# Moving part of the gate matrix onto three DMA engines, and the last pieces of wo back to full rows

## The chip, the cores and the metric

One core of a Trainium2 chip. The metric is the device time of one execution in microseconds (us); the kernel is timed in several executions beside the other kernel on the same chip. A profile shows one execution; its span is some 1.3 us shorter than the time on the clock (194.8 against 196.06 in the profile of the kernel before). On one core there is no second die to compare with, so a run is called fast when it lies within 1.5% of the fastest of its kernel.

## The reference

One decoding step: attention over the last 4,096 positions of a K and a V cache, beside a gated feed-forward layer, mixed by a gate g.

```python
def _A_ref(x, k_cache, v_cache, wq, wo):              # x: 4 x 1 x 512
    q = (x @ wq).reshape(B, Sq, 32, 128)...           # wq: 512 x 4096
    k = k_cache[:, :, Sk - 4096:, :]                  # 4 x 8 x 4096 x 128, bf16: 33.5 MB; v the same
    p = softmax(q k^T * Dh ** -0.5); o = p v
    return o.reshape(B, Sq, 4096) @ wo                # wo: 4096 x 512

def _B_ref(x, W_gate, W_up, W_down):                  # 512 x 1792, 512 x 1792, 1792 x 512
    gate = x @ W_gate; up = x @ W_up
    return (relu(gate) * up) @ W_down

g = sigmoid((x * gate_w).sum(-1))
return g * _A_ref(x, ...) + (1 - g) * _B_ref(x, ...)
```

Every byte of K, V and the five matrices is read once: 81.0 MB.

## The kernel before

Everything goes through four 4 MiB slots of the on-chip memory in one fixed order of loads, all issued by SP: wq, x, gate_w, K0, K1, V0, then K and V of the eight sets in turn, the gate and up matrices, the last V, the down matrix, and wo in five pieces. DVE transposes K, PE makes scores and PV (the weighted sums of V). PE is the matrix engine, DVE the vector engine, ACT the scalar engine; SP only issues loads. At the end PE does, in this order: the last PV, the down projection (`hg`), `fold` (16 matmuls that add up and regroup the attention output), and, once DVE has made `oq` from it, 64 matmuls with wo. The last 64 KB of wo are cut into loads of 123, 3 and 2 partitions, which leave eight completion marks (191.87 to 192.39) where a load of all 128 partitions leaves sixteen. Their packets of 512 B run in three trains, about 23.7 ns apart in each, so they are taken to go onto three DMA engines only; these are called the low three below. The sixteen marks of a full load lie close together at first (22.30 to 22.84 for the first K). The parts that the change touches:

```python
WO_PIECES = ((0, 34), (34, 52), (52, 60), (60, 63), (63, 64))   # in units of 256 columns, 64 KB each
LOW3 = (0, 123, 126, 128)

def _dma_order():
    o = [("wq",), ("x",), ("gw",), ("k", 0), ("k", 1), ("v", 0)]
    for s in range(2, NSET):
        o += [("k", s), ("v", s - 1)]
    return o + [("wg",), ("wu",), ("v", NSET - 1), ("wd",)] + [("wo", p) for p in range(len(WO_PIECES))]

    def wo_rows(p):      # the last piece in three loads of 123, 3 and 2 partitions
        return [slice(a, b) for a, b in zip(LOW3, LOW3[1:])] if p == len(WO_PIECES) - 1 else [slice(0, 128)]
# ... sync:
            elif k == "wg":
                load(("WG",), "d_wg", Wg, B_W_gate.rearrange("(p t) f -> p (t f)", t=4), waits=w)
            elif k == "wo":
                lo, hi = WO_PIECES[it[1]]
                wo = A_wo.rearrange("(p i) c -> p (i c)", i=32)
                for n, r in enumerate(wo_rows(it[1])):
                    load(("WO", it[1], n), f"d_wo{it[1]}", Wo[r, OW * lo:OW * hi], wo[r, OW * lo:OW * hi], waits=w)
# ... tensor:
        def XT():        # x and gate_w transposed, four 5-column pieces
            for q in range(4):
                tp(bk[:, 6 * q:6 * q + 5], xsb[0:5, q:q + 509:4], identb[0:5, 0:5], ...)
        def GU():        # gate and up: four row groups q, four column blocks j of 448
            for n, (W, key) in enumerate(((Wg, "WG"), (Wu, "WU"))):
                for q in range(4):
                    for j in range(4):
                        mm(banks[scb(fill)][32 * j:32 * j + 4, 0:448], xT[:, 5 * q:5 * q + 4],
                           W[:, FF * q + 448 * j:FF * q + 448 * j + 448], q == 0, q == 3, ...)
        def WO(p):
            for x in range(lo, hi):
                mm(banks[ACC][OR * j:OR * j + 4, 0:OW], oq[:, i, :], Wo[:, OW * x:OW * x + OW], False, i == 31,
                   waits=w if x == lo else (), ...)
# ... vector and scalar evict one half of the output each:
        def FIN():       # DVE waits for the last piece, ACT for the last but one
            E.op(lambda: v.tensor_copy(osum[:, OW:2 * OW], banks[ACC][OR:OR + 4, 0:OW]), ...)
```

Of the kernel before, what the change touches and what calls it, by code (L numbers as in the profile page):

```python
# [16 lines left out]
FF = 1792  # L17
# [7 lines left out]
OUTT = 2  # L25
OW = 512 // OUTT
OR = 128 // OUTT
WO_PIECES = ((0, 34), (34, 52), (52, 60), (60, 63), (63, 64))
LOW3 = (0, 123, 126, 128)

class _Plan:

# [70 lines left out]
def _alloc(nc, ctx):  # L103
    R = {}

    def sb(name, shape, dt):
        R[name] = ctx.enter_context(nc.sbuf_tensor(name, shape, dt))

    sb("slots", [128, NSLOT, 16384], BF16)
    sb("kt", [128, 4, 4096], BF16)  # L110
    sb("sc", [128, 2048], BF16)
    sb("pe", [128, 2048], BF16)
    sb("pT", [128, 2, 2048], BF16)
    sb("qblk", [128, NSET, 2, 144, 2], BF16)
    sb("xsb", [5, 512], BF16)
    sb("xT", [128, 20], BF16)
    sb("osb", [128, NSET, 512], BF16)
    sb("oq", [128, 32, 4], BF16)
    sb("identb", [128, 128], BF16)
    sb("identf", [128, 128], FP32)  # L120
    sb("ones", [128, 128], FP32)
    sb("ee", [16, 128], BF16)
    sb("e4", [16, 128], BF16)
    sb("rfold", [128, 128], FP32)
    sb("grpb", [128, 128], BF16)
    sb("own8", [128, 8], FP32)
    sb("scl", [128, 8], FP32)
    sb("maskl", [128, 128], BF16)
    sb("maskr", [128, 512], BF16)
    sb("maskf", [128, 512], BF16)  # L130
    sb("gwB", [128, 4, 128], BF16)
    sb("fold", [128, 4, 4, 64], BF16)
    sb("mx4", [128, 4], FP32)
    sb("rd32", [128, 8, 4], BF16)
    sb("negmax", [128, 2], FP32)
    sb("rowsum", [128, NSET], FP32)
    sb("recip", [128, 4, 4], FP32)
    sb("ge", [128, 2, 4], FP32)
    sb("gp", [128, 2, 4], FP32)
    sb("gg", [128, 2, 4], FP32)  # L140
    sb("hg", [128, 14, 4], BF16)
    sb("osum", [4, 512], BF16)
    R["psum"] = ctx.enter_context(nc.psum_tensor("bank", [128, 8, 512], FP32))
    return R

# [11 lines left out]


def _dma_order():
    o = [("wq",), ("x",), ("gw",), ("k", 0), ("k", 1), ("v", 0)]  # L160
    for s in range(2, NSET):
        o += [("k", s), ("v", s - 1)]
    return o + [("wg",), ("wu",), ("v", NSET - 1), ("wd",)] + [("wo", p) for p in range(len(WO_PIECES))]


def _slots():

    frees = [[] for _ in range(NSLOT)]
    at, wait = {}, {}
    turn = 0  # L170
    for it in _dma_order():
        k = it[0]
        if k in ("x", "gw") or (k == "wo" and it[1] > 0):
            continue
        if k == "wu":
            at[it] = at[("wg",)]
            wait[it] = wait[("wg",)]
            continue
        n = turn % NSLOT
        turn += 1  # L180
        at[it] = n
        wait[it] = list(frees[n])
        frees[n] = {"k": [("E", "KT", it[-1], 3)], "v": [("PV", it[-1])], "wq": [("Q", 1)], "wg": [("GU", 1)], "wd": [], "wo": []}[k]
    return at, wait


def _program(nc, plan, R, aps):
# [5 lines left out]
    xsb, xT, osb, oq = R["xsb"], R["xT"], R["osb"], R["oq"]  # L193
    identb, identf, ones = R["identb"], R["identf"], R["ones"]
    mx4, rd32, negmax, rowsum, recip = R["mx4"], R["rd32"], R["negmax"], R["rowsum"], R["recip"]
    ge, gp, gg, osum = R["ge"], R["gp"], R["gg"], R["osum"]
    consts = {"mask": R["maskf"], "grp": R["grpb"], "rfold": R["rfold"]}

    at, slot_wait = _slots()
# [39 lines left out]
        n = scf[key] - NSC  # L239
        return [("E",) + sck[n]] if n >= 0 else [("INIT",)]  # L240

    def wo_rows(p):

        return [slice(a, b) for a, b in zip(LOW3, LOW3[1:])] if p == len(WO_PIECES) - 1 else [slice(0, 128)]

    def set_of(s):
        return s % 4, s // 4
# [4 lines left out]
    def sync(e):  # L252
# [5 lines left out]
        for it in _dma_order():  # L258
# [6 lines left out]
            elif k == "wq":  # L265
                load(("WQ",), "d_wq", slot("wq"), A_wq.rearrange("(p t) f -> p (t f)", t=4), waits=w)
            elif k == "wg":
                load(("WG",), "d_wg", Wg, B_W_gate.rearrange("(p t) f -> p (t f)", t=4), waits=w)
            elif k == "wu":
                load(("WU",), "d_wu", Wu, B_W_up.rearrange("(p t) f -> p (t f)", t=4), waits=w)  # L270
            elif k == "wd":
# [2 lines left out]
            elif k == "wo":  # L274
                lo, hi = WO_PIECES[it[1]]
                wo = A_wo.rearrange("(p i) c -> p (i c)", i=32)
                for n, r in enumerate(wo_rows(it[1])):
                    load(("WO", it[1], n), f"d_wo{it[1]}", Wo[r, OW * lo:OW * hi], wo[r, OW * lo:OW * hi], waits=w)
            else:
                b, qq = set_of(it[1])  # L280
                src = (A_k_cache if k == "k" else A_v_cache)[b, 4 * qq:4 * qq + 4, SK - WIN:SK, :]
                load((k.upper(), it[1]), f"d_{k}{it[1] % 3}", slot(*it), src.rearrange("h (r c) d -> r h (c d)", r=32),
                     waits=w)
# [32 lines left out]
    def tensor(t):  # L316
# [16 lines left out]
        def XT():  # L333
            bk = bankb[tr(("XT",))]
            for q in range(4):
                tp(bk[:, 6 * q:6 * q + 5], xsb[0:5, q:q + 509:4], identb[0:5, 0:5], ev=("XT",) if q == 3 else None,
                   waits=tr_free(("XT",)) + [("X",), ("GW",), ("IDB",)])

        def Z():
            for q in range(4):  # L340
# [65 lines left out]
        def GU():  # L406
            for n, (W, key) in enumerate(((Wg, "WG"), (Wu, "WU"))):
                fill = ("GU", n)
                for q in range(4):
                    for j in range(4):  # L410
                        mm(banks[scb(fill)][32 * j:32 * j + 4, 0:448], xT[:, 5 * q:5 * q + 4],
                           W[:, FF * q + 448 * j:FF * q + 448 * j + 448], q == 0, q == 3,
                           ev=fill if (q, j) == (3, 3) else None, pos=(0, 32 * j),
                           waits=sc_free(fill) + [(key,)] if (q, j) == (0, 0) else ())

        def FFN():
            for i in range(14):
# [5 lines left out]

        def WO(p):
            lo, hi = WO_PIECES[p]
            w = [("WO", p, n) for n in range(len(wo_rows(p)))] + [("E", "OQ")]
            for x in range(lo, hi):
                i, j = x // OUTT, x % OUTT
                mm(banks[ACC][OR * j:OR * j + 4, 0:OW], oq[:, i, :], Wo[:, OW * x:OW * x + OW], False, i == 31,
# [8 lines left out]
    for it in order:  # L438
# [3 lines left out]
        elif k == "CONST":  # L442
            act.append(("ECONST", it[1]))
        elif k == "XT":
            dve.append(("EXT",))
            act.append(("GWB",))
        elif k == "Z":
            act.append(("GE",))
# [33 lines left out]
    def vector(v):  # L482
        E = _Eng(plan, v, "dve")

        def INIT():
            E.op(lambda: v.memset(qblk[:, :, :, :, :].rearrange("p s h c e -> p (s h c e)"), 0.0), ev=("QZ",))  # L486
            E.op(lambda: v.memset(R["psum"][:, SCB[0]:ACC + 1, :].rearrange("p k c -> p (k c)"), 0.0), ev=("INIT",))

        def EKT(s, f):
            w = [("K", s)] + ([("SC", s - 1, f)] if s else [])  # L490
            E.op(lambda: v.transpose(kt[:, f, :].bitcast(FP32), slot("k", s)[:, 4096 * f:4096 * f + 4096].bitcast(FP32)),  # L491
                 ev=("E", "KT", s, f), waits=w)

        def EXT():
            E.op(lambda: v.tensor_copy(xT[:, :].rearrange("p (q c) -> p q c", q=4), bankb[tr(("XT",))][:, 0:24].rearrange("p (q c) -> p q c", q=4)[:, :, 0:5]), ev=("E", "XT"), waits=[("XT",)])  # L495

        def EQ(n):
            key = ("Q", n)
# [41 lines left out]

        def EPT(s):
            E.op(lambda: v.transpose(pT[:, s % 2, :], pe[:, :]), ev=("E", "PT", s),  # L542
                 waits=[("EXP", s)] + ([("PV", s - 2)] if s >= 2 else []))

        def ERS(g):
            key = ("RS", g)
# [29 lines left out]
        def FIN():  # L576
            E.op(lambda: v.tensor_copy(osum[:, OW:2 * OW], banks[ACC][OR:OR + 4, 0:OW]), ev=("OSUM", 1),  # L577
                 waits=[("WOP", len(WO_PIECES) - 1)])

        fns = dict(INIT=INIT, EKT=EKT, EXT=EXT, EQ=EQ, G=G, EQT=EQT, ESC=ESC, MAX=MAX, ESW=ESW, EPT=EPT, ERS=ERS, EOQ=EOQ, H=H,  # L580
                   EHT=EHT, FIN=FIN)
        for it in dve:
            fns[it[0]](*it[1:])
# [1 line left out]
    def scalar(a):  # L585
# [35 lines left out]

        def FIN():
            E.op(lambda: a.activation(osum[:, 0:OW], banks[ACC][0:4, 0:OW], ACTF.Copy), ev=("OSUM", 0),
                 waits=[("WOP", len(WO_PIECES) - 2)])

        fns = dict(ECONST=ECONST, GWB=GWB, EQ=EQ, GE=GE, RELU=RELU, EXP=EXP, NORM=NORM, FIN=FIN)
        for it in act:
# [31 lines left out]
```

## Time and profile before

| | before |
|---|---|
| time, median of 3 | 196.12 us (196.02 to 196.21) |
| span of the profile, granted TensorE clock | 194.8 us, 0.912 |
| data moved, rate over the span | 81.01 MB, 416 GB/s |
| DMA queue's share of sixteen engines' span | 97.3% |
| busy: PE, DVE, ACT | 62%, 64%, 14% |

The prediction below shows the page, the end of the chain of waits and the PE timeline of the tail. The waits (engine and line, what it waited for, total us, times, longest us):

```profile
DVE kt L491 <- DMA slots<-in_A_k_cache_dram: 28.0, 6, 5.2
PE bank L320 <- DMA slots<-in_A_v_cache_dram: 5.7, 1, 5.7
```

DVE has 28 us in which it waits for K: it has slack, DMA has none. The second line is PE waiting for the last V, at the end. What PE then does, in the timeline (start, duration, engine, line, operation):

```profile
178.49 5.03 PE L320 MATMUL bank<-slots,pT 128*64 128x512 bf16 x32 [5.70 <-DMA slots<-in_A_v_cache_dram]
183.45 1.69 PE L320 MATMUL bank<-slots,hg 128*4 128x256 bf16 x28
185.07 1.93 PE L320 MATMUL bank<-osb,fold 128*64 128x256 bf16 x16
...
187.04 0.88 DVE L555 TENSOR_TENSOR oq<-bank,recip 64x128 bf16<-64x128 f32 x2 [12.25 <-PE bank L320]
188.05 1.75 PEld L320 LDWEIGHTS bank<-slots,oq 128*4 128x4 bf16 x34 [1.31 <-DMA slots<-in_A_wo_dram]
```

A third reading is not a view but the trace's completion marks: a load of all 128 partitions leaves sixteen as it lands, as many as the page counts DMA engines, and so a mark is read here as one engine's part that has landed. A load that leaves fewer has one more soon after SP has issued it (at 8.67 us for the first side load, whose issue ended at 8.25), which is not counted. Marks carry no engine's name: that two loads met on one engine is read from which marks come late. They are quoted in us from the span's start, and a mark's place is where it stands in their order. An instruction page (often just a page) is a packet of 16,384 B on queue q8, which the profile lists as instruction (5 packets, 0.08 MB, in the kernel before); the prediction shows when they come.

### The profile page before, as it was taken

How to read it: one execution, taken by the hardware profiler on the slowest of the kernel's cores; microseconds unless marked ns; L12 is line 12 of the kernel's file. 1: busy time of each engine (PE TensorE's matmuls, PEld its weight loads, DVE VectorE, ACT ScalarE, POOL GpSimd, SP SyncE). 2: the span in 40 equal slices, each digit the busy share in tenths (PEclk: the TensorE clock that was granted, in tenths of full speed). 3: DMA queues.
4: the chain of work that ended last, by engine and by line, in shares of the span. 5: the costliest groups of instructions: out<-in, count | busy, mean ns of one | idle time of the engine just before them, and what ended most of it. 6: DMA issues, size and time to landing. Idle time of an engine off the chain costs nothing.

```text
span 194.8 us, 1734 instructions
## 1 busy us (share of the span) xinstructions
PE 120.6 (62%) x723; PEld 50.6 (26%) x723; DVE 124.1 (64%) x153; ACT 27.5 (14%) x34; POOL 9.5 (5%) x25
## 2 busy tenths in 40 slices
PE   0209279474943894686468943894586466743974
PEld 0003123121411341242112411341142122311562
DVE  6103769999399809980998199819981998370010
ACT  2213000040130013001300130013001300420100
POOL 7830000000000000000000000000000000000000
PEclk9999958999999797899876999697999889997899
DMA  6999999999999999999999999999999999999992
GB/s 215 431 432 431 437 437 431 431 427 451 431 437 437 446 427 424 431 437 431 431 431 431 427 424 437 444 437 431 431 431 421 431 395 427 470 431 384 425 404 90
DMA packets 3616, 81.10 MB, mean 416 GB/s; under 512 B 401, under 2 KB 666, under 8 KB 794
## 3 DMA queue, kind: packets, MB, share of 16 engines
q1 hardware_dynamic: 3610, 81.01, 97.3%
q8 instruction: 5, 0.08, 0.2%
q14 instruction: 1, 0.01, 0.0%
HBM read 81.01 MB, written 0.00 MB: 416 GB/s over the span
## 4 chain that ended last, share of the span: by engine, by line
DMA 54%; DVE 31%; PE 9%; issue 4%; SPq 0%; ACT 0%
DMA slots<-in_A_k_cache_dram 38%; DVE kt L491 21%; DMA slots<-in_A_wo_dram 10%; PE bank L320 7%; DMA xsb<-in_A_x_dram 6%; DVE sc L527 5%; DVE qblk L517 1%; PE bank L324 1%; DVE pT L542 1%; DVE rd L531 1%; SPq L256 0%; DVE negmax L537 0%; ACT gwB L600 0%; DVE osum L577 0%; DVE mx L527 0%
## 5 line engine op out<-in xcount | busy, mean ns | idle before, releaser
L491 DVE STREAM_TRANSPOSE kt<-slots 128x2048 f32<-128x2048 f32 x32 | 73.7, 2305 | 28.1 <-DMA slots<-in_A_k_cache_dram 28.0
L320 PE MATMUL bank<-kt,qblk 128*128 128x512 bf16 x256 | 72.1, 434 | 27.9 <-DVE kt L491 27.9
L320 PEld LDWEIGHTS bank<-kt,qblk 128*128 128x128 bf16 x256 | 25.2, 107 | 69.7 <-DVE kt L491 36.0
L320 PE MATMUL bank<-slots,pT 128*64 128x512 bf16 x256 | 32.3, 410 | 5.7 <-DMA slots<-in_A_v_cache_dram 5.7
L619 ACT ACTIVATE pe<-sc,negmax 128x2048 bf16<-128x2048 bf16 x8 | 16.0, 2002 | 60.1 <-DVE negmax L537 60.1
L527 DVE CUSTOM_DVE_ANT_0 sc<-bank,maskf 128x512 bf16<-128x512 f32 x32 | 21.0, 658 | 3.8 <-PE bank L320 3.7
L320 PEld LDWEIGHTS bank<-slots,pT 128*64 128x64 bf16 x256 | 15.1, 118 | 23.2 <-issue 13.4
L542 DVE STREAM_TRANSPOSE pT<-pe 128x2048 bf16<-128x2048 bf16 x8 | 18.5, 2312 | 2.2 <-ACT pe L619 2.2
L604 ACT ACTIVATE osb<-bank 128x512 bf16<-128x512 f32 x8 | 4.8, 597 | 81.5 <-PE bank L320 81.5
L320 PE MATMUL bank<-rd,grpb 128*128 128x32 bf16 x8 | 1.6, 194 | 22.1 <-DVE rd L531 22.1
L555 DVE TENSOR_TENSOR oq<-bank,recip 64x128 bf16<-64x128 f32 x2 | 0.9, 434 | 12.3 <-PE bank L320 12.2
L320 PEld LDWEIGHTS bank<-rd,grpb 128*128 128x128 bf16 x8 | 0.8, 98 | 25.7 <-DVE rd L531 25.7
L495 DVE COPY xT<-bank 128x20 bf16<-128x20 bf16 x1 | 0.2, 171 | 8.0 <-PE bank L324 8.0
L320 PE MATMUL bank<-slots,oq 128*4 128x256 bf16 x64 | 4.0, 272 | 2.0 <-DMA slots<-in_A_wo_dram 2.0
L320 PE MATMUL bank<-slots,xT 128*4 128x512 bf16 (+1 forms) x64 | 5.0, 467 | 0.0
L320 PE MATMUL bank<-maskr,maskl 128*128 128x512 bf16 x1 | 0.6, 609 | 5.9 <-POOL maskr L296 5.9
L517 DVE TENSOR_SCALAR qblk<-bank 32x64 uint32<-32x64 uint32 x16 | 2.9, 215 | 2.1 <-PE bank L324 2.1
L324 PE MATMUL bank<-identb,xsb 5*128 5x5 bf16 x4 | 0.3, 168 | 5.7 <-DMA xsb<-in_A_x_dram 5.7
L577 DVE CAST osum<-bank 4x256 bf16<-4x256 f32 x1 | 0.4, 418 | 5.2 <-PE bank L320 5.2
L320 PEld LDWEIGHTS bank<-slots,oq 128*4 128x4 bf16 x64 | 2.5, 84 | 3.5 <-DMA slots<-in_A_wo_dram 2.9
L296 POOL TENSOR_SCALAR_AFFINE_SELECT fold<-fold 128x256 bf16<-128x256 bf16 x8 | 3.3, 417 | 1.1
L486 DVE MEMSET qblk<- 128x2304 uint32 x1 | 2.0, 1978 | 1.3 <-PEq L644 1.3
(59 smaller groups left out, 40.3 us busy)
## 6 DMA issues: line engine op xcount, KB each, us to landing
slots<-in_A_k_cache_dram SPq DMA_DIRECT2D x8, 4096.0 KB, 25.1
slots<-in_A_v_cache_dram SPq DMA_DIRECT2D x8, 4096.0 KB, 30.5
slots<-in_A_wq_dram SPq DMA_DIRECT2D x1, 4096.0 KB, 12.4
slots<-in_A_wo_dram SPq DMA_DIRECT2D x1, 2176.0 KB, 17.1
slots<-in_B_W_gate_dram SPq DMA_DIRECT2D x1, 1792.0 KB, 19.7
slots<-in_B_W_up_dram SPq DMA_DIRECT2D x1, 1792.0 KB, 23.6
slots<-in_B_W_down_dram SPq DMA_DIRECT2D x1, 1792.0 KB, 18.5
slots<-in_A_wo_dram SPq DMA_DIRECT2D x1, 1152.0 KB, 19.5
```

The source lines that it names most:

```text
L296: op(lambda: e.affine_select(dst, src, pattern, cmp, fill, base=base, channel_multiplier=mult), ev)
L320: E.op(lambda: t.matmul(out_, lhsT, rhs, start=start, stop=stop, tile_position=pos, skip_group_check=True), ev=ev, waits=waits)
L324: E.op(lambda: t.transpose(out_, in_, idn), ev=ev, waits=waits)
L486: E.op(lambda: v.memset(qblk[:, :, :, :, :].rearrange("p s h c e -> p (s h c e)"), 0.0), ev=("QZ",))
L491: E.op(lambda: v.transpose(kt[:, f, :].bitcast(FP32), slot("k", s)[:, 4096 * f:4096 * f + 4096].bitcast(FP32)), ev=("E", "KT", s, f), waits=w)
L517: E.op(lambda dst=dst, r=r, g=g: v.tensor_scalar(dst, src[r, g, 0:B, :, :], 0, None, op0=ALU.bitwise_or), ev=("E",) + keys[1] if (q, g) == ...
L527: E.op(lambda: v.tensor_tensor_reduce(sc[:, 512 * f:512 * f + 512], banks[scb(key)], R["maskf"][:, :], 1.0, -3.0e38, ALU.add, ALU.max, mx4 ...
L531: E.op(lambda: v.tensor_tensor(rd32[:, :, :], bc(R["own8"][:, :].unsqueeze(2), 2, 4), bc(mx4[:, :].unsqueeze(1), 1, 8), ALU.mult), ev=("MA ...
L542: E.op(lambda: v.transpose(pT[:, s % 2, :], pe[:, :]), ev=("E", "PT", s), waits=[("EXP", s)] + ([("PV", s - 2)] if s >= 2 else []))
L555: E.op(lambda g=g, r=r: v.tensor_tensor(oq[r, :, :].rearrange("p i b -> p b i"), banks[tr(key)][0:64, 128 * g:128 * g + 128].rearrange("p ...
L604: E.op(lambda: a.activation(osb[:, s, :], ob(s), ACTF.Copy), ev=("NORM", s), waits=[("PV", s)])
L619: E.op(lambda: a.activation(pe[:, :], sc[:, :], ACTF.Exp, bias=negmax[:, s % 2:s % 2 + 1], scale=SCALE, accum_out=rowsum[:, s:s + 1]), ev= ...
```

## The change

Its intent, as the marks suggest: by the end some engines are late and others early, and the early ones can be given more. An equal load cannot do that, but the loads of 123, 3 and 2 partitions left eight marks, and loads laid out in rows of 3, 3 and 2 were meant to do the same. So 448 columns of one row in four of the gate matrix (114,688 B) are taken out of the equal load and put on three engines early on; in return wo's last 64 KB go back to all sixteen, in full rows. PE then needs the matching rows of x, hence the extra copies, transposes and gate matmuls.

```diff
-WO_PIECES = ((0, 34), (34, 52), (52, 60), (60, 63), (63, 64))
-LOW3 = (0, 123, 126, 128)
+SIDE_F, SIDE_J = 1344, 6
+SIDE = ((3, 5, 0, 0, 0), (3, 5, 60, 32, 0), (2, 1, 120, 0, 5))   # engines, rows each partition, first row, partition, place
+WO_PIECES = ((0, 35), (35, 52), (52, 59), (59, 62), (62, 64))
...
-    o = [("wq",), ("x",), ("gw",), ("k", 0), ("k", 1), ("v", 0)]
+    o = [("wq",), ("x",), ("gw",), ("k", 0), ("side", 0), ("side", 1), ("side", 2), ("k", 1), ("v", 0)]
...
+        e, j, p, q, j0 = SIDE[n]
+        src = wg_all[p:p + 4 * e * j, 3 * FF + SIDE_F:4 * FF]
+        return side[q:q + 4 * e, j0:j0 + j, :], src.rearrange("(r e) f -> e r f", e=e)
...
-                load(("WG",), "d_wg", Wg, ...)
+                load(("WG",), "d_wg", Wg[:, 0:3 * FF + SIDE_F], wg_all[:, 0:3 * FF + SIDE_F], waits=w)
+            elif k == "side":
+                load(("SIDE", it[1]), f"d_side{it[1]}", *side_of(it[1]), waits=[("SZ",)])
...
+            for j in range(SIDE_J):
+                tp(bk[:, 6 * (4 + j):6 * (4 + j) + 5], xg[:, j, :], identb[0:5, 0:5], ...)
...
-                for q in range(4):
+                for q in range(4 if n else 3 + SIDE_J):      # block j = 3 of the last group comes from side, six matmuls
...
+            E.op(lambda: v.memset(xg, 0.0), ev=("XGZ",))
+            E.op(lambda: v.memset(side[...].bitcast(FP32), 0.0), ev=("SZ",))
...  # ACT's half of the output now waits for the last piece, as DVE's does;
...  # hg and osum move into gwB and xsb to make room (cut)
```

More of the change, by code (lines that the diff above doesn't have):

```diff
@@ L115, in _alloc @@
     sb("xsb", [5, 512], BF16)
-    sb("xT", [128, 20], BF16)
+    sb("xT", [128, 20 + 5 * SIDE_J], BF16)
+    sb("side", [128, SIDE_J, FF - SIDE_F], BF16)
     sb("osb", [128, NSET, 512], BF16)
@@ L140, in _alloc @@
     sb("gg", [128, 2, 4], FP32)
-    sb("hg", [128, 14, 4], BF16)
-    sb("osum", [4, 512], BF16)
+    R["hg"] = R["gwB"][:, 0, 0:56].rearrange("p (i b) -> p i b", i=14)
     R["psum"] = ctx.enter_context(nc.psum_tensor("bank", [128, 8, 512], FP32))
@@ L172, in _slots @@
         k = it[0]
-        if k in ("x", "gw") or (k == "wo" and it[1] > 0):
+        if k in ("x", "gw", "side") or (k == "wo" and it[1] > 0):
             continue
@@ L195, in _program @@
     mx4, rd32, negmax, rowsum, recip = R["mx4"], R["rd32"], R["negmax"], R["rowsum"], R["recip"]
-    ge, gp, gg, osum = R["ge"], R["gp"], R["gg"], R["osum"]
+    ge, gp, gg, side = R["ge"], R["gp"], R["gg"], R["side"]
+    osum = xsb[0:4, :]
+    xg = pT[0:5, 0, 0:128 * SIDE_J].rearrange("p (j q) -> p j q", j=SIDE_J)
     consts = {"mask": R["maskf"], "grp": R["grpb"], "rfold": R["rfold"]}
@@ L240, in sc_free, with side_of, side_x @@
         return [("E",) + sck[n]] if n >= 0 else [("INIT",)]
-    def wo_rows(p):
-        return [slice(a, b) for a, b in zip(LOW3, LOW3[1:])] if p == len(WO_PIECES) - 1 else [slice(0, 128)]
+    wg_all = B_W_gate.rearrange("(p t) f -> p (t f)", t=4)
+    def side_of(n):
+        e, j, p, q, j0 = SIDE[n]
+        src = wg_all[p:p + 4 * e * j, 3 * FF + SIDE_F:4 * FF]
+        return side[q:q + 4 * e, j0:j0 + j, :], src.rearrange("(r e) f -> e r f", e=e)
+    def side_x(n):
+        e, j, p, q, j0 = SIDE[n]
+        src = xsb[0:5, 4 * p:4 * p + 16 * e * j].rearrange("p (r j e t) -> p j e r t", r=4, j=j, e=e, t=4)[:, :, :, :, 3]
+        return xg[:, j0:j0 + j, q:q + 4 * e].rearrange("p j (e r) -> p j e r", e=e), src
     def set_of(s):
@@ L267, in sync @@
             elif k == "wg":
-                load(("WG",), "d_wg", Wg, B_W_gate.rearrange("(p t) f -> p (t f)", t=4), waits=w)
+                load(("WG",), "d_wg", Wg[:, 0:3 * FF + SIDE_F], wg_all[:, 0:3 * FF + SIDE_F], waits=w)
+            elif k == "side":
+                load(("SIDE", it[1]), f"d_side{it[1]}", *side_of(it[1]), waits=[("SZ",)])
             elif k == "wu":
@@ L276, in sync @@
                 wo = A_wo.rearrange("(p i) c -> p (i c)", i=32)
-                for n, r in enumerate(wo_rows(it[1])):
-                    load(("WO", it[1], n), f"d_wo{it[1]}", Wo[r, OW * lo:OW * hi], wo[r, OW * lo:OW * hi], waits=w)
+                load(("WO", it[1]), f"d_wo{it[1]}", Wo[:, OW * lo:OW * hi], wo[:, OW * lo:OW * hi], waits=w)
             else:
@@ L335, in XT @@
             for q in range(4):
-                tp(bk[:, 6 * q:6 * q + 5], xsb[0:5, q:q + 509:4], identb[0:5, 0:5], ev=("XT",) if q == 3 else None,
+                tp(bk[:, 6 * q:6 * q + 5], xsb[0:5, q:q + 509:4], identb[0:5, 0:5],
                    waits=tr_free(("XT",)) + [("X",), ("GW",), ("IDB",)])
+            for j in range(SIDE_J):
+                tp(bk[:, 6 * (4 + j):6 * (4 + j) + 5], xg[:, j, :], identb[0:5, 0:5], ev=("XT",) if j == SIDE_J - 1 else None,
+                   waits=[("XG",)])
         def Z():
@@ L408, in GU @@
                 fill = ("GU", n)
-                for q in range(4):
+                for q in range(4 if n else 3 + SIDE_J):
                     for j in range(4):
-                        mm(banks[scb(fill)][32 * j:32 * j + 4, 0:448], xT[:, 5 * q:5 * q + 4],
-                           W[:, FF * q + 448 * j:FF * q + 448 * j + 448], q == 0, q == 3,
-                           ev=fill if (q, j) == (3, 3) else None, pos=(0, 32 * j),
-                           waits=sc_free(fill) + [(key,)] if (q, j) == (0, 0) else ())
+                        of_side = n == 0 and q > 2 and 448 * j >= SIDE_F
+                        if q > 3 and not of_side:
+                            continue
+                        c = 5 * q + 5 * of_side
+                        x = 448 * j - SIDE_F
+                        rhs = side[:, q - 3, x:x + 448] if of_side else W[:, FF * q + 448 * j:FF * q + 448 * j + 448]
+                        last = q == (2 + SIDE_J if of_side else 3)
+                        w = sc_free(fill) + [(key,)] if (q, j) == (0, 0) else []
+                        if n == 0 and (q, j) == (3, 0):
+                            w = [("SIDE", g) for g in range(len(SIDE))]
+                        mm(banks[scb(fill)][32 * j:32 * j + 4, 0:448], xT[:, c:c + 4], rhs, q == 0, last,
+                           ev=fill if last and j == 3 else None, pos=(0, 32 * j), waits=w)
         def FFN():
@@ L425, in WO @@
             lo, hi = WO_PIECES[p]
-            w = [("WO", p, n) for n in range(len(wo_rows(p)))] + [("E", "OQ")]
+            w = [("WO", p), ("E", "OQ")]
             for x in range(lo, hi):
@@ L444, in _program @@
         elif k == "XT":
-            dve.append(("EXT",))
+            dve += [("XG",), ("EXT",)]
             act.append(("GWB",))
@@ L485, in INIT @@
         def INIT():
+            E.op(lambda: v.memset(xg, 0.0), ev=("XGZ",))
             E.op(lambda: v.memset(qblk[:, :, :, :, :].rearrange("p s h c e -> p (s h c e)"), 0.0), ev=("QZ",))
             E.op(lambda: v.memset(R["psum"][:, SCB[0]:ACC + 1, :].rearrange("p k c -> p (k c)"), 0.0), ev=("INIT",))
+            E.op(lambda: v.memset(side[:, :, :].rearrange("p j f -> p (j f)").bitcast(FP32), 0.0), ev=("SZ",))
         def EKT(s, f):
@@ L492, in EKT, with XG @@
                  ev=("E", "KT", s, f), waits=w)
+        def XG():
+            for n in range(len(SIDE)):
+                E.op(lambda n=n: v.tensor_copy(*side_x(n)), ev=("XG",) if n == len(SIDE) - 1 else None,
+                     waits=[("X",), ("GW",), ("XGZ",)])
         def EXT():
-            E.op(lambda: v.tensor_copy(xT[:, :].rearrange("p (q c) -> p q c", q=4), bankb[tr(("XT",))][:, 0:24].rearrange("p (q c) -> p q c", q=4)[:, :, 0:5]), ev=("E", "XT"), waits=[("XT",)])
+            E.op(lambda: v.tensor_copy(xT[:, :].rearrange("p (q c) -> p q c", c=5), bankb[tr(("XT",))][:, 0:24 + 6 * SIDE_J].rearrange("p (q c) -> p q c", c=6)[:, :, 0:5]), ev=("E", "XT"), waits=[("XT",)])
         def EQ(n):
@@ L542, in EPT @@
             E.op(lambda: v.transpose(pT[:, s % 2, :], pe[:, :]), ev=("E", "PT", s),
-                 waits=[("EXP", s)] + ([("PV", s - 2)] if s >= 2 else []))
+                 waits=[("EXP", s)] + ([("PV", s - 2)] if s >= 2 else [("XT",)]))
         def ERS(g):
@@ L578, in FIN @@
                  waits=[("WOP", len(WO_PIECES) - 1)])
-        fns = dict(INIT=INIT, EKT=EKT, EXT=EXT, EQ=EQ, G=G, EQT=EQT, ESC=ESC, MAX=MAX, ESW=ESW, EPT=EPT, ERS=ERS, EOQ=EOQ, H=H,
+        fns = dict(INIT=INIT, XG=XG, EKT=EKT, EXT=EXT, EQ=EQ, G=G, EQT=EQT, ESC=ESC, MAX=MAX, ESW=ESW, EPT=EPT, ERS=ERS, EOQ=EOQ, H=H,
                    EHT=EHT, FIN=FIN)
@@ L623, in FIN @@
             E.op(lambda: a.activation(osum[:, 0:OW], banks[ACC][0:4, 0:OW], ACTF.Copy), ev=("OSUM", 0),
-                 waits=[("WOP", len(WO_PIECES) - 2)])
+                 waits=[("WOP", len(WO_PIECES) - 1)])
         fns = dict(ECONST=ECONST, GWB=GWB, EQ=EQ, GE=GE, RELU=RELU, EXP=EXP, NORM=NORM, FIN=FIN)
```

## The prediction

> **What bounds the kernel now.** I read the page first, then the list of transfers, then the chain of waits in order of time, then the tail's timeline, and last the completion marks that the trace keeps for each transfer. The page, lines of its parts 1 to 4:
>
> ```profile
> PE 120.6 (62%) x723; PEld 50.6 (26%) x723; DVE 124.1 (64%) x153; ACT 27.5 (14%) x34; POOL 9.5 (5%) x25
> ...
> DMA  6999999999999999999999999999999999999992
> ...
> q1 hardware_dynamic: 3610, 81.01, 97.3%
> q8 instruction: 5, 0.08, 0.2%
> ...
> DMA 54%; DVE 31%; PE 9%; issue 4%; SPq 0%; ACT 0%
> ```
>
> No compute engine is above 64%, but the DMA row is 9 in every slice but the first and last, and the data queue fills 97.3% of sixteen engines' span. 81.01 MB at about 431 GB/s (the GB/s row) is 188 us; what is left of the 194.8 us span is start and tail. So the kernel is bound by bytes on the DMA engines, and the change moves no bytes away: it moves them between engines.
>
> The chain of waits in order of time, its last pieces (start, duration, what):
>
> ```profile
> 171.74 20.41 DMA slots<-in_A_wo_dram
> 192.16 0.04 issue
> 192.20 0.87 PE bank L320 x12
> 193.07 0.02 issue
> 193.09 0.42 DVE osum L577
> ```
>
> The end is: wo's third piece lands at 192.16, twelve matmuls, one 0.42 us eviction, the output. The PE timeline of the same stretch:
>
> ```profile
> 188.07 2.02 PE L320 MATMUL bank<-slots,oq 128*4 128x256 bf16 x34 [1.06 <-DMA slots<-in_A_wo_dram]
> 190.83 1.15 PE L320 MATMUL bank<-slots,oq 128*4 128x256 bf16 x18 [0.73 <-DMA slots<-in_A_wo_dram]
> 192.20 0.82 PE L320 MATMUL bank<-slots,oq 128*4 128x256 bf16 x12 [0.23 <-DMA slots<-in_A_wo_dram]
> ```
>
> Each batch waits for its piece, so the landing of wo, not PV or the output projection, sets the end; a matmul here costs 0.82/12 = 0.068 us.
>
> The page cannot show which engine is late. The completion marks can: sixteen per full transfer. Counted from the span's start, the first K block's marks lie within 22.30 to 22.85. The last V block's: eleven at 176.6 to 177.2, five at 177.7 to 178.4. The piece of wo with columns 60 to 63: ten at 190.7 to 191.2, six at 191.9 to 192.60. So by the end six engines are up to 1.4 us behind the other ten. The packets say why: the five packets of 16,384 B on q8 (instructions) start at 40.2, 73.0, 111.7, 148.2 and 182.1, take 1.02 to 1.07 us each, and after each of them one more mark is late by that much; an 8,192 B packet of q14 at 63.3 makes a smaller one. The kernel before already uses this: its last piece of wo (64 KB in packets of 512 B) is cut into 123, 3 and 2 partitions, and its marks (eight) lie at 191.87 to 192.40, just before the last of the laggards.
>
> [...] 123, 3 and 2 partitions leave 3 + 3 + 2 = 8 marks. [...] at the five fetches PE had started 205, 447, 710, 969 and 1222 instructions, about 254 apart.
>
> **The change part by part.**
> 1. *Bytes of the thirteen other engines.* Before, 64 KB lay on the low three only; after, it is 128 x 896 B = 114,688 B. The even part falls by 49,152 B, or 3,072 B an engine: at 431/16 = 26.9 GB/s that is 0.11 us. The laggards' last mark goes from 192.60 to about 192.48.
> 2. *Bytes of the low three.* Removed: 43 rows of 512 B on two engines, 42 on the third. Their packets in the trace follow at about 23.7 ns on an engine: 1.0 us. Added: 44, 44 and 40 rows of 896 B. Packets of 4,096 B take 159 ns and of 512 B 23.7 ns; the line through both is 4.4 ns + 0.0378 ns per B, so 38 ns for 896 B. [...] Their last marks before were, by order and spacing, about 192.1, 192.2 and 192.4; after: 192.6 to 193.1, middle 192.85. So the low three would be loaded slightly past the laggards. This is an estimate, and the weakest term.
> 3. *The tail.* Before, 12 matmuls stood behind the third piece's landing (0.87 us). After, the last piece is two matmuls on all sixteen engines: last landing + 0.04 + 0.15 to 0.2 + 0.02 + 0.42 = landing + 0.65. With 192.48 the last eviction ends at 193.13 (before 193.51), with 192.85 at 193.50, with 193.1 at 193.75. The scalar engine's half of the output now also waits for the last piece: 0.37 us beside 0.42, no cost.
> 4. *Start.* DVE clears two more tiles: the 128x2304 u32 memset takes 1.98 us, so the 1344-wide one some 1.2, and the small one some 0.5; they end near 7.2 us, and DVE's next work is at 13.53. Three small copies (0.17 us as the xT copy) and six 5-column transposes (0.07 us each) come between x and xT: +0.5 to 0.9 us before the first K transposes. The SP queue holds K1 and V0 until the memset is done, some 4 us later than now; wq and K0 keep the engines busy until 22.
> 5. *Middle.* Five more matmuls of the gate in the stretch before the last V lands (PE idles 5.70 us there): hidden. The low three now lag from the 24th us instead of at the end; K blocks land up to 1.9 us later until the laggards are as late. DVE has 28.0 us of waits for K, and a K load is issued 23 to 25 us before it lands with 9.7 us of its own: over a block is always queued, so no engine starves, and a shifted start costs nothing.
>
> Sum: -0.4 (laggards still set the end) to +0.25 us (low three do); I put it at -0.1.
>
> **The rivals.**
> (a) *The low three do not become the bound*: for it, 896 B rows spread over a long busy stretch may cost only their bytes (33 ns), 1.46 us, about the lead of 1.4; time 195.75.
> (b) *They do, and more than reckoned*: rows of 512 B show the fixed cost per packet[...]; 196.3 to 196.5.
> (c) *A sixth instruction page.* PE has 1459 records; the change adds 11 matmuls or transposes, 22 records, and a few waits. The next page boundary extrapolates to 1222 + 254 = 1476 of then about 1483: it would be fetched in the last microsecond. On an engine that is done it costs nothing; on one that still has rows of the last piece, up to 1.05 us: 196.6 to 197. Against: ten engines are done early.
> (d) *The side loads go to one engine*: [...] about 200, slower by 2%. [...]
> (e) [...] A 3-partition load now holds SP for 10.3 us near the end:
>
> ```profile
> 173.05 11.67 SPq L256 DMA_DIRECT2D slots<-in_A_wo_dram  x2
> ```
>
> with some 80 rows then queued on a low engine. The side loads put 44 rows there at the start, about 71 with wq, K0, K1 and V0; V0's issue may wait, perhaps to 18 us, but its data is needed at 32. No cost.
>
> **Range and chances.** Predicted 196.0 us: the 196.12 of before less 0.1. Case (a) gives 195.75, case (b) 196.4, case (c) a tail above; runs of one kernel differ by 0.2. So 195.5 to 196.5. Over 2% either way is 3.9 us: a gain would need bytes that are not removed, a loss needs (d) or starvation. Faster 0.01, within 2% 0.975, slower 0.015.
>
> **What would show it.** The marks of the last wo piece are the test: its latest near 192.5 with three marks not among them says (a); three marks of their own at 192.6 to 193.1 say the sum's middle. The side loads should leave 3, 3 and 2 marks[...]. PE should have 2 matmuls after the last landing and end 0.2 us after it. xT should be ready 0.5 to 0.9 us later, and the first wait for K that follows (now 72.55) end within 0.5 us of it. I am wrong if the DMA row shows a gap in the first half, if a sixth instruction packet falls before the last landing and delays it, or if the end of PV rather than wo sets the tail.

In part 2 the low three came to +0.4 to +0.8 us. The 38 ns a row of the packet line alone gives +0.4 to +0.6 (40 and 44 rows are 1.5 and 1.7 us, less the 1.0 and the 0.11); the upper end took a longer time for a row that starts at byte 13,440, which no trace had shown. From the whole range come 192.6 to 193.1 and the middle 192.85, and from these the sum: -0.4 to +0.25, put at -0.1, which makes 196.0. The "about 200" of (d) was worked out with the longer row too; with 38 ns it is an estimate of 4.9 us less 1.4, or 199.6. That the side loads would take 3, 3 and 2 engines is left with the eight marks of the kernel before as its ground. What held SP for 10.3 us in (e) is not shown.

## The result

| | before | changed |
|---|---|---|
| time, median | 196.12 us, 6 runs (196.02 to 196.21) | 195.98 us, 6 runs (195.79 to 196.22) |
| ratio of fast runs | | 0.9993, 95% interval 0.998 to 1.0006 |
| span, granted clock | 194.8 us, 0.912 | 194.6 us, 0.912 |

A ratio is the mean time of one kernel's fast runs over that of the other's of the same rounds, so it is not quite the ratio of the medians quoted. The prediction was 196.0, within 2%; the change is no clear gain. The page after:

```profile
PE 123.0 (63%) x734; PEld 51.5 (26%) x734; DVE 126.5 (65%) x158; ACT 27.5 (14%) x34; POOL 9.5 (5%) x25
...
DMA  6999999999999999999999999999999999999993
...
q1 hardware_dynamic: 3754, 81.01, 97.4%
q8 instruction: 6, 0.10, 0.2%
...
DMA 53%; DVE 31%; PE 10%; issue 5%; ACT 0%; SPq 0%
```

Same bytes, same share; 11 more matmuls and transposes, 5 more DVE records, and six instruction packets instead of five. The end of the chain of waits:

```profile
172.30 18.27 DMA slots<-in_A_wo_dram
190.57 0.04 issue
190.61 2.17 PE bank L335 x29
192.78 0.02 issue
192.81 0.42 DVE xsb L611
```

The last eviction starts at 192.81 instead of 193.09. The chain names an earlier piece than before (190.57) because PE's waits inside the last 29 matmuls are short; the timeline shows them on the weight loads:

```profile
190.61 0.85 PEld L335 LDWEIGHTS bank<-slots,oq 128*4 128x4 bf16 x17 [0.48 <-DMA slots<-in_A_wo_dram]
190.61 2.15 PE L335 MATMUL bank<-slots,oq 128*4 128x256 bf16 x29 [0.19 <-DMA slots<-in_A_wo_dram]
191.68 0.30 PEld L335 LDWEIGHTS bank<-slots,oq 128*4 128x4 bf16 x7 [0.22 <-DMA slots<-in_A_wo_dram]
192.19 0.09 PEld L335 LDWEIGHTS bank<-slots,oq 128*4 128x4 bf16 x3 [0.21 <-DMA slots<-in_A_wo_dram]
192.49 0.08 PEld L335 LDWEIGHTS bank<-slots,oq 128*4 128x4 bf16 x2 [0.21 <-DMA slots<-in_A_wo_dram]
```

Batches of 7, 3 and 2 each start 0.04 us after a last mark (191.64, 192.15, 192.45). The completion marks of the last full piece of wo:

```
before, columns 60 to 63 : ten at 190.70 to 191.23, six at 191.88 to 192.60; low-three piece, eight at 191.87 to 192.39
changed, columns 62 to 64: seven at 190.56 to 191.04, nine at 191.90 to 192.45
```

Three more engines are late, and the last is 0.15 us earlier. The other 0.13 of the 0.28 us by which the eviction moved is the work behind the last mark: two matmuls instead of four (0.36 us from the mark to the eviction instead of 0.49). The side loads leave 3, 3 and 2 marks of their own (23.14 to 24.34 us), as predicted. The start, from both timelines, before:

```profile
13.53 0.17 DVE L495 COPY xT<-bank 128x20 bf16<-128x20 bf16 x1 [8.01 <-PE bank L324]
```

and after:

```profile
6.18 1.18 DVE L516 MEMSET side<- 128x1344 f32 x1 [0.27 <-issue]
...
14.22 0.19 DVE L529 COPY xT<-bank 128x50 bf16<-128x50 bf16 x1 [0.41 <-PE bank L339]
```

xT is ready 0.71 us later. It reaches no further than the first waits for K, which shrink to this line (28.0 before):

```profile
L520 DVE STREAM_TRANSPOSE kt<-slots 128x2048 f32<-128x2048 f32 x32 | 73.7, 2305 | 25.0 <-DMA slots<-in_A_k_cache_dram 25.0
```

### The profile page after: what moved, and what is told of

Same layout as the page of the kernel before. It is cut to its first block, busy times and chain, and to the rows that moved or that the text cites. A ratio compares the mean times of both kernels' runs of the same rounds, so it can differ in the third digit from the quotient of the medians.

```text
span 194.6 us, 1764 instructions
## 1 busy us (share of the span) xinstructions
PE 123.0 (63%) x734; PEld 51.5 (26%) x734; DVE 126.5 (65%) x158; ACT 27.5 (14%) x34; POOL 9.5 (5%) x25
## 4 chain that ended last, share of the span: by engine, by line
DMA 53%; DVE 31%; PE 10%; issue 5%; ACT 0%; SPq 0%
DMA slots<-in_A_k_cache_dram 38%; DVE kt L520 21%; DMA slots<-in_A_wo_dram 9%; PE bank L335 9%; DMA xsb<-in_A_x_dram 6%; DVE sc L561 5%; DVE qblk L551 1%; PE bank L339 1%; DVE pT L576 1%; DVE rd L565 1%; DVE negmax L571 0%; ACT gwB L634 0%; DVE pT L525 0%; SPq L270 0%; DVE xsb L611 0%
## 5 line engine op out<-in xcount | busy, mean ns | idle before, releaser
L335 PE MATMUL bank<-slots,xT 128*4 128x512 bf16 (+1 forms) x63 | 6.2, 491 | 0.0
L525 DVE COPY pT<-xsb 5x60 bf16<-5x60 bf16 (+1 forms) x3 | 0.5, 213 | 6.0 <-DMA xsb<-in_A_x_dram 6.0
L571 DVE TENSOR_REDUCE negmax<-bank 128x1 f32<-128x32 f32 x8 | 1.5, 192 | 2.0 <-PE bank L335 2.0
```

Of the source, the lines that this page charges most:

```text
L335: E.op(lambda: t.matmul(out_, lhsT, rhs, start=start, stop=stop, tile_position=pos, skip_group_check=True), ev=ev, waits=waits)
L571: E.op(lambda: v.tensor_reduce(negmax[:, s % 2:s % 2 + 1], banks[tr(key)][:, 0:32], AXIS.X, ALU.min), ev=("E",) + key, waits=[key])
```

## The experiments

The theory: the latest DMA engine sets the end, each engine's lateness is its own bytes plus the instruction pages fetched over it, and the low three were filled up to the level of the others. Rivals: the rearranged tail is the whole gain; the side load is hidden in the start; the lag has another cause than the pages; the start's delay is paid.

Twelve runs. "Last mark" is that of wo's last full piece in the profiled run. side_late, the two stairs and rep_before ran on another chip than the other eight; each ratio is against runs of the kernel before in the same session.

| kernel | time, median | ratio to before, 95% | last mark |
|---|---|---|---|
| tail_only | 196.41 | 1.0011 (0.9999 to 1.0023) | 193.09 |
| side_only | 196.96 | 1.0044 (1.0031 to 1.0057) | 193.32 (low three) |
| side6 | 196.75 | 1.0045 (1.0016 to 1.0075) | 193.38 |
| side8 | 196.58 | 1.0019 (1.0006 to 1.0032) | 193.33 |
| rep_after (changed kernel) | 195.96 | 0.9987 (0.9973 to 1.0001) | 192.55 |
| side_late | 195.87 | 0.9988 (0.9974 to 1.0001) | 192.48 |
| start_delay | 196.17 | 1.0001 (0.9987 to 1.0016) | 192.56 |
| no_pages (wrong result) | 195.66 | 0.9972 (0.996 to 0.9985) | 191.88 |
| no_pages_side (wrong result) | 196.30 | 1.0016 (0.9998 to 1.0034) | 192.48 |
| stair_a, stair_b (probe) | 204.22, 203.68 | one run each | 200.40, 200.27 |
| rep_before (kernel before) | 196.33 | one run | 192.82 |

### The two halves of the change alone

**tail_only**: the kernel before with the new pieces of wo.

```diff
-WO_PIECES = ((0, 34), (34, 52), (52, 60), (60, 63), (63, 64))
+WO_PIECES = ((0, 35), (35, 52), (52, 59), (59, 62), (62, 64))      # and every piece in full rows
```

> The kernel before with only the wo pieces of the change (0-35, 35-52, 52-59, 59-62, 62-64, all in full rows), no side load. My theory (the slowest DMA engine sets the end): the 64 KB that lay on the low three are now spread over all sixteen, 4,096 B more an engine = +0.15 us, so the last mark goes from 192.60 to about 192.75; two matmuls behind it instead of the rest of twelve saves about as much; net 0.0, 196.1 to 196.2 us, ratio to before 1.000. Rival (the shorter tail behind the last landing is the whole gain and the side load does nothing): 195.9, as fast as the changed kernel, last mark not later than 192.5.

196.41 us (196.08 to 196.71), slower than the changed kernel (195.75 to 196.22 in its ten runs): in this program the tail alone gains nothing. My figure was 0.2 too low. Five late marks stood at 191.78 to 192.52, as reckoned or earlier; the sixth was at 193.09, because the page at 182.5 fell on an engine that was already 0.3 us behind the slowest of the early ones (187.00 would have been its place in the first piece, 188.55 it was). So the loss is one page on an unlucky engine and not the missing side load: without that mark the last would be 192.52, level with the 192.45 and 192.55 of the changed kernel. This run alone therefore doesn't rule the rival out; what the side load gains apart from where the pages fall was not separated.

**side_only**: the changed kernel with the pieces of wo of before, low-three piece included.

```diff
-WO_PIECES = ((0, 35), (35, 52), (52, 59), (59, 62), (62, 64))
+WO_PIECES = ((0, 34), (34, 52), (52, 60), (60, 63), (63, 64))      # and LOW3, wo_rows as in the kernel before
```

> The changed kernel with the wo pieces of before, the last one again on the low three engines in 512 B packets, so that these carry both extra loads. My theory: the low three were level with the laggards in the changed kernel, so they end 1.0 to 1.4 us after them; marks of the low-three piece at 193.3 to 193.9 us, time 197.0 to 197.4, ratio to before 1.005 to 1.007. Rival (the side load is hidden anyway): 13 engines carry 7 KB less than before, so 196.0 or less and those marks before 192.6.

196.96 us, just under what was expected (197.0 to 197.4; ratio 1.0044 against 1.005 to 1.007). The low-three marks came at 192.87 to 193.32, up to 1.2 us after the last of the equal piece (192.11); the range of 193.3 to 193.9 was set too late, only the last mark reached it. That an extra load on three engines shows in the time says that they had no room left. The side load is not hidden.

### More engines

**side6** and **side8**: the side load widened to 896 columns, laid out for six engines, and to 1,344, laid out for eight. "Lowest" and the numbers 3 to 7 in the expectations are labels for the engines that such loads take beside the low three; no record shows an engine's number. The page of side8 counts 425 packets under 512 B against 409 in no_pages, 16 more, or eight for each of its two loads.

```diff
-SIDE_F, SIDE_J = 1344, 6
-SIDE = ((3, 5, 0, 0, 0), (3, 5, 60, 32, 0), (2, 1, 120, 0, 5))
+SIDE_F, SIDE_J = 896, 3                                            # side6
+SIDE = ((6, 2, 0, 0, 0), (6, 2, 48, 32, 0), (6, 1, 96, 0, 2), (2, 1, 120, 32, 2))
+SIDE_F, SIDE_J = 448, 2                                            # side8
+SIDE = ((8, 2, 0, 0, 0), (8, 2, 64, 32, 0))
```

> The changed kernel with the side load widened to 896 columns and to the six lowest engines (20 or 24 rows of 1,792 B on each, about 1.4 to 1.7 us by the packet line). The even part falls by 7,168 B an engine against the changed kernel = 0.27 us. If engines 3 to 5 fetch no instructions: 195.7 us, last mark near 192.2, eleven late marks. If one of them also fetches instruction pages: it ends 1.1 to 1.4 us after the others, 197.0 us. Rival (the DMA engines do not set the end): 196.0 either way.

> The changed kernel with the side load widened to 1344 columns and to the eight lowest engines (16 rows of 2,688 B on each, 1.7 us). The even part falls by 14,336 B an engine against the changed kernel = 0.53 us. If engines 3 to 7 fetch no instructions: 195.5 us. If one of them does: its mark is 1.1 to 1.4 us behind and the time is 196.7 to 197.0. Rival (the DMA engines do not set the end): 196.0.

Both slower than the changed kernel: the branch "one of them also fetches", each a little under the time expected for it (197.0, and 196.7 to 197.0). One of the six executions of side6 took 198.77 us at a span of 195.9; what happened outside the span is not recorded, and it widens the interval. In side8 fifteen marks of the last piece stood at 190.16 to 191.91, half a microsecond before the changed kernel's last, as the smaller equal part promised, and one at 193.33. That one could be followed back: it was 0.43 us behind the other low engines after the side load (34.40 against 33.97 at K1; one mark was 0.41 behind already at K0, 22.96 against 22.55) and fell 1.0 us further just after the 8,192 B instruction packet at 47.3. In side6 two marks were late twice, from the packets at 46.5 and 112.1. Here one engine hit twice cost more than all the others gained.

### The pages

**no_pages**: tail_only with one matmul where there were many, so that PE has 178 records, with every load, wait and DVE instruction kept; the result is wrong. **no_pages_side**: the same cut in the changed kernel.

```diff
-            for t in range(2):
-                for h in range(2):
-                    for e in range(2):                              # eight matmuls for one score block
+            mm(bk, qblk[:, s, 0, 16:144, 0], kv[:, 0, :, 0, :, 0], True, True, ev=key, waits=w)
...                                                                  # PV 32 -> 1, GU 16 -> 1, FFN 28 -> 2, OQ 16 -> 1, WO 64 -> 6, Q 32 -> 2
```

> Wrong result on purpose. The kernel of tail_only with most matmuls left out (one per score block, one per PV block, and so on), every load, every wait and all DVE and ACT work kept, so that PE has some 190 records instead of 1459 and fetches no instruction page during the run. My theory (pages make engines late): no packets of 16,384 B, all marks of the last wo piece within about 1 us, the latest at 191.3 to 191.9 instead of 193.09; 194.6 to 195.2 us, ratio to before 0.992 to 0.995. Rival (the lag comes from elsewhere, or PE sets the pace): five or six late marks remain and the last is not before 192.3; 196 us.

> Wrong result on purpose. The changed kernel (side load on the low three) with the same matmuls left out. My theory: exactly three late marks, the low three, the latest at 192.2 to 192.5, as late as in the changed kernel, and thirteen early ones up to 191.6; 195.6 to 195.9 us, so slower than no_pages by 0.6 to 1.2 us. Rival (the side load hides early in the kernel): as fast as no_pages or 0.1 us faster.

The page of no_pages, its parts on DMA:

```profile
DMA  6999999999999999999999999999999999999992
GB/s 223 432 433 432 432 432 432 432 432 432 432 432 434 432 432 432 432 432 432 432 432 432 432 432 432 432 432 432 432 432 425 432 429 425 436 432 422 425 407 104
...
q1 hardware_dynamic: 3618, 81.01, 97.6%
q14 instruction: 1, 0.01, 0.0%
```

There is no q8 row: no 16,384 B packet was fetched. The GB/s row, which in slices 2 to 30 jumps between 424 and 451 in the kernel before, stands at 432 to 434 there. All sixteen marks of the last piece lie within 190.81 to 191.88, 1.2 us earlier than in tail_only; the latest is the one that the single 8,192 B packet delayed. So the late engines are the pages' doing. (The cut takes PE's work away together with the pages; that each page by itself moves one engine is what the probe below shows.) In no_pages_side the marks were twelve at 190.55 to 190.82, one at 191.73 (the 8,192 B packet), and 192.28, 192.31, 192.48. Those three are the low three without any page, and they are as late as the latest of the changed kernel. Both expectations on the marks held, but for the one mark at 191.73, which was to be at 191.6 at most. One of the four executions of no_pages_side took 197.22 us at a span of 194.9, again outside the span. The times did not: both came out about 0.4 to 0.5 us over the range, though their difference (0.64 us) is inside what was expected. Part of that is seen: time less span is 1.43 and 1.52 us here and 1.27 in tail_only, and the two matmuls after the last landing take some 0.4 us. The rest I leave open.

**stair_a, stair_b**: a probe for which engines fetch pages: fifteen extra loads of n rows of 8,192 B, n from 15 to 1, which are meant to leave each engine at its own place. The page of stair_a counts 529 packets under 512 B against 409 in no_pages, whose loads are otherwise the same (in the first trace these packets, 401, are all of 4 B and as many as the landing marks); the 120 more are 15 + 14 + ... + 1, one for each extra row. That the engines of a shorter load are among those of a longer one is assumed. Then one engine gets 15 rows, the next 14, and so on; the expectation numbers them 0, 1, ... in that order. These are labels and not numbers that a record shows.

```diff
-    o = [..., ("k", 0), ("k", 1), ("v", 0)]
+    o = [..., ("k", 0)] + [("st", n) for n in range(15, 0, -1)] + [("k", 1), ("v", 0)]
```

> A probe, slower on purpose: the kernel of tail_only with fifteen extra loads of n rows of 8,192 B, n = 15 down to 1, into a tile that is not yet in use, so that [...] the engines are spread by 0.31 us each: the marks of every later load then name their engine. My theory (each instruction page delays one engine by about 1.1 us): each of the five packets of 16,384 B moves exactly one engine's place by 1.0 to 1.2 us; engines 0 to 2 are not among them, as in five traces so far; at least one of 3 to 7 is, as in side8. The slowest engine is 0, 4.6 us behind: about 199.2 us. Rival (the lag is shared or has another cause): several engines move by parts of it.

> The same kernel again. If the engine of a page is a property of the program, the same five engines move at the same pages; if it is a matter of the run, others do.

What it was built for, it showed. Each page moved one mark, and by about 1.5 us (for instance from a place of 47.01 to 48.56 at the first page of stair_a), not by the 1.0 to 1.2 expected; the 8,192 B packet moved one by 0.8 to 1.0. Counted from the late end, which is 0, the places were 14, then 5 and 6, 8 or 9, and 10 or 11 for the pages and 2 or 3 for the small one, each to within one neighbour, the same in both runs. So the engine of a page did not change between two runs of one program. In side8, another program, all five pages fell on engines without a side load; if the eight that have one there are places 0 to 7 here, which is not shown, the engine did change between programs. What sets it stays open. The time was 5 us over: all sixteen engines were 4.8 us later, also the one without extra rows, and packets of 8,192 B that took 0.31 us at first took up to 1.08. The windows view (stretch, length, busy of the engines, granted clock, DMA share, GB/s):

```profile
22.00:23.00 1.00, 0.00 (x0) 0.00 (x0) 0.96 (x7) 0.00 (x0) 0.00 (x0) 1.00 1.51 270
23.00:24.00 1.00, 0.00 (x0) 0.00 (x0) 0.35 (x2) 0.00 (x0) 0.00 (x0) 1.00 0.91 131
24.00:25.00 1.00, 0.00 (x0) 0.00 (x0) 0.83 (x1) 0.00 (x0) 0.00 (x0) 1.00 1.12 188
```

The engines are busy nearly all the time (the share is 0.91 to 1.51, over 1 where packets overlap) and move 131 to 270 GB/s, where the usual is 431. Why is not shown: the loads are of 15 rows and fewer, and all fifteen also read the same rows of memory; nothing here tells whether it was either.

### The place of the load and the start

**side_late**: the side loads queued before the gate matrix instead of after K0. **start_delay**: 3.5 us of needless DVE work between x and xT.

```diff
-    o = [..., ("k", 0), ("side", 0), ("side", 1), ("side", 2), ("k", 1), ("v", 0)]
-    return o + [("wg",), ...
+    o = [..., ("k", 0), ("k", 1), ("v", 0)]                                        # side_late
+    return o + [("side", 0), ("side", 1), ("side", 2), ("wg",), ...
+            E.op(lambda: v.memset(kt[:, 0:2, :]....bitcast(FP32), 0.0), waits=[("X",), ("GW",)])   # start_delay
```

> The changed kernel with the side loads queued just before the gate matrix (about 145 us) instead of after the first K block. My theory (what counts is each engine's total): same as the changed kernel, 195.9 to 196.1, last mark 192.4 to 192.6, low three late only from about 155 us on. Rival (the place matters, because the early side load holds back K1 and V0 or is hidden in the start): differs by 0.5 us or more.

> The changed kernel with one needless clearing of half the transposed-K tile (about 3.5 us on DVE) put between the landing of x and the new copies, so that xT is ready some 3.5 us later. My theory (start is off the path): unchanged, 195.8 to 196.2, first waits for K shorter by what was added. Rival (the 0.7 us that the change added at the start is paid): 198 to 199.5.

side_late: 195.87 us, last mark 192.48, the low three late only from 159 us on. In this kernel totals count, not places in the queue. start_delay: xT at 18.6, the last mark still at 192.56, and 196.17 us. The rival's 198 is out. Still, its profiled run, 196.32, was 0.4 longer than that of the changed kernel, with the same last mark, and this is where the second chain to the end comes in, beside the landing of wo: last V, PV, down projection, fold, oq, 64 matmuls.

### The second chain

**rep_after** and **rep_before**: both kernels again, unedited.

> The changed kernel once more, unedited, to narrow its interval and for a second trace. My theory: 195.9 to 196.1, ratio to before 0.998 to 1.000, no clear difference; three engines late by the side load, and five or six instruction packets; if the engines that fetch instructions differ from run to run, the late marks are grouped otherwise than in the first trace, and where one falls on a low engine a mark is a further 1.1 us late and the run near 197. Rival (the engines are fixed): the same nine late marks at 191.9 to 192.45.

> The kernel before once more, unedited, for a second trace: 196.0 to 196.3; last mark of the piece with columns 60 to 63 between 192.4 and 192.8; six late marks if no two pages fall on one engine, as in the first trace.

rep_after came as expected, nine late marks up to 192.55. In rep_before time and last mark came a hair above what was expected (196.33 against 196.3, 192.82 against 192.8), with six late marks as in the first trace, and the profile's chain no longer runs through it:

```profile
149.41 29.33 DMA slots<-in_A_v_cache_dram
178.74 0.14 issue
178.88 9.70 PE bank L320 x76
...
188.60 0.43 DVE oq L555
...
189.04 0.45 DVE oq L555
...
189.63 3.70 PE bank L320 x64
193.33 0.02 issue
193.35 0.42 DVE osum L577
```

From the last V's landing to the end there is no DMA in it: 76 matmuls, oq, 64 matmuls in one piece. In the first trace the 64 were held up three times by wo. Here they start 1.56 us later than there, for two reasons: the last V landed 0.39 us later (178.74 against 178.35), and the last PV took 6.20 us instead of 5.03, under a lower granted clock. The windows view of 178 to 190 us in rep_before:

```profile
178.00:190.00 12.00, 10.05 (x84) 6.11 (x86) 0.87 (x2) 0.60 (x1) 0.00 (x0) 0.75 0.99 414
```

and in the first trace of the same kernel:

```profile
178.00:190.00 12.00, 10.45 (x110) 6.76 (x110) 0.87 (x2) 0.60 (x1) 0.00 (x0) 0.86 0.99 415
```

0.75 against 0.86, and 84 matmuls started in it instead of 110. Cut finer, the clock from 182 to 184 us was 0.50 in rep_before and 1.00 in the first trace. start_delay's profile is of the same kind (0.73, and 0.50 from 182 to 184; PV 6.52 us):

| profiled run | time | last mark | granted clock, 178 to 190 | wo matmuls start | last eviction starts |
|---|---|---|---|---|---|
| before | 196.06 | 192.60 | 0.86 | 188.07 | 193.09 |
| rep_before | 196.33 | 192.82 | 0.75 | 189.63 | 193.35 |
| changed | 195.92 | 192.45 | 0.86 | 188.30 | 192.81 |
| rep_after | 195.93 | 192.55 | 0.86 | 188.42 | 192.91 |
| side_late | 195.87 | 192.48 | 0.87 | 187.99 | 192.84 |
| start_delay | 196.32 | 192.56 | 0.73 | 189.59 | 193.29 |

In start_delay this cost time: PE ended 0.70 us after the last mark (193.26), where 0.33 is enough in the changed kernel, and the eviction started 0.38 us later than in rep_after at the same last mark. That accounts for its 0.4 us. In rep_before it cost next to nothing: PE ended 0.51 us after the last mark, and in the first trace of the same kernel 0.47. The landing alone would have let the eviction start at 192.82 + 0.49 = 193.31 (an estimate by the first trace), against 193.35; so its 0.27 us over the first profile are mostly the later landing (0.22). With the clock that low the evictions of the two kernels start at 193.35 and 193.29, so the rearranged loads have little to gain in such a run. Which unprofiled runs were of this kind is not recorded.

## Why the prediction was right

1. *Equal part, -0.11 us.* The last mark moved from 192.60 and 192.82 to 192.45 and 192.55 in two traces each, so by 0.05 to 0.37. The term lies in that spread, but the scatter of a trace is as large as the term. The same arithmetic can be checked where no pages disturb: from no_pages to no_pages_side the equal part falls by 7,168 B an engine, 0.27 us at 26.9 GB/s, and the earliest mark moved from 190.81 to 190.55, by 0.26.
2. *Low three, last marks at 192.6 to 193.1.* Mis-sized, as the prediction feared: no_pages_side has them alone at 192.28 to 192.48, level with the laggards, so neither rival (a) nor (b) but the border between. The added rows took 0.75 us for 20, 37.5 ns each, which is the line through the packets (38); the longer row of the estimate's upper end did not come. (That line mixes a duration, 159 ns, with a spacing, 23.7. The recorded durations alone are 27 ns for 512 B, 159 for 4,096 and 41 for 896, which is again on the line through the first two.) And the removed piece was worth more than its packets' 1.0 us: its last mark came 0.83 us after the start of its last packet, against 0.48 us for the side load. Why is not shown: the side load is three loads in a row as well. These two together are about the size of the 0.4 us between estimate and measurement. Two slips in the working changed little: its own terms give 192.5 to 193.2 instead of 192.6 to 193.1, and it read each instruction page as making one mark late by the length of the packet (1.02 to 1.07 us), where each moved a mark by about 1.5.
3. *Tail, landing + 0.65 us.* It was 192.45 to 193.23, 0.78: the last two matmuls took 0.29 us from their start at 192.49, not 0.15 to 0.2. So the two errors, one late and one early, partly cancelled, and the eviction ended at 193.23 where 193.50 was the middle. That the sum held to 0.02 us in the time is luck of that kind, within a range that had room for it.
4. *Start, +0.5 to 0.9 us, no cost.* 0.71; and 3.5 us more changed no landing. The memsets ended at 7.36 (predicted near 7.2).
5. *Middle.* The first wait for K that DMA ends moved from 72.55 to 72.86, inside the 0.5 allowed.
6. *Rivals.* (c) A sixth page did come, at 191.76, and delayed no mark: the steps from the piece before to the last were 0.28 to 0.34 us for all sixteen, taken by rank. (d) did not happen, the marks were 3, 3 and 2. (e) SP was not held: V0 was issued at 10.4.
7. "The landing of wo, not PV, sets the end" held in the traces of the changed kernel and in the first trace of the one before. The prediction listed its failure among what would make it wrong; it did happen, at a cost of some 0.04 us in rep_before and 0.38 in start_delay. It may be one reason why a quarter of a microsecond in the trace is 0.14 in the medians; that is not shown, since only profiled runs have marks.

Whether 0.9993 and 0.9987 are a true gain of a tenth of a per cent is not settled: both intervals reach 1. No version tried beats the changed kernel clearly; side_late (0.9988) is its equal.

## What to carry to other kernels

A saturated DMA row (97.3% here) hides the question of which engine is last: read the completion marks of the last loads one by one, and add up bytes per engine, small packets and instruction pages (here about 1.5 us each) included. Load that was moved to the early engines gained here only up to the level of the next late one (192.45 and 192.55), and in side6 and side8 an engine hit twice gave it all back (193.38 and 193.33). And before tuning a tail, ask for the second chain to it and for the clock under which it was traced: here the two met within 0.2 us in one run and crossed in the next.
